# Wider source reads for contiguous loads, and V loads of half the size, in a two-attention kernel

## The chip, the cores and the metric

The kernel runs on one core of one Trainium2 chip. The metric is the device time of one execution in microseconds; a version's time is the median of several executions. A profiled execution also leaves a trace: the instructions of each engine (TensorE for matrix products, called PE in the profile; VectorE, DVE; ScalarE, ACT; GpSimd, POOL; SyncE, SP), the DMA packets, and what released each wait. The core has 16 DMA engines. They move data between main memory (HBM) and the on-chip buffer SBUF, which has 128 partitions; here a partition is also called a row of the destination.

## The reference

Two attention blocks over the same batch shape are computed, and their outputs are laid side by side. Block A has 4 heads of K and V that are shared by 8 query heads each; block B has 32 heads of its own.

```python
def _A_ref(x, k_cache, v_cache, wq, wo):          # x (16, 32, 1024), k and v (16, 4, 1024, 128)
    q = (x @ wq).reshape(B, Sq, 32, 128).transpose(0, 2, 1, 3)
    k = jnp.repeat(k_cache, 8, axis=1)
    v = jnp.repeat(v_cache, 8, axis=1)
    scores = jnp.einsum("bhqd,bhkd->bhqk", q, k) * (128 ** -0.5)
    p = _softmax(scores, axis=-1)
    o = jnp.einsum("bhqk,bhkd->bhqd", p, v)
    return o.transpose(0, 2, 1, 3).reshape(B, Sq, 4096) @ wo
...
a = _A_ref(A_x, A_k_cache, A_v_cache, A_wq, A_wo)
b = _B_ref(B_x, B_k_cache, B_v_cache, B_wq, B_wo)  # the same, with k and v (16, 32, 1024, 128), no repeat
return jnp.concatenate([a, b], axis=-1)            # (16, 32, 2048)
```

All of it is in bfloat16. K and V of block B are 134.2 MB each; K and V of block A, and the query weights and the output weights (both blocks together), are 16.8 MB each. Nearly all of the 338 MB that are read is read once.

## The kernel before

Work is cut into 128 steps. A step of block B ("quad B") takes two batches and two heads: 32 queries of each of the four pairs make the 128 rows of one tile of scores, 128 x 1024. A step of block A ("quad A") takes one batch and four query heads that share one head of K and V. A step in `build` does for B, and likewise for A:

- load K (`st_dmaK`) and V (`st_dmaV`) some steps ahead. For B, K is two loads of 512 KB (L748, one per batch, each partition 4096 B) into one of 8 slots of `KB_sb`, and V two loads of 512 KB (L761, one per batch) into one of 3 slots of `VB_sb`. A load of V for B fills, in each partition, two stretches of 2048 B, one for each head. For A, K (L743, `KA_sb`) and V (L755, `VA_sb`) are one load of 256 KB each, 2048 B to a partition, into one of 2 slots.
- K of B is transposed in place by DVE (L782), K of A by PE (L774);
- scores on PE (L823 for B, L803 for A), the row maximum on DVE (L833), the exponential on ACT (L846), the transpose of P on PE (L858) and its eviction to `PT_sb` (L525);
- P times V on PE (L888 for B, named PVB, four pieces of 32 matmuls in a step; L880 for A), the division by the row sum (L904 on ACT or L905 on DVE), and a transpose of the result on PE (L910).

Between these stand the query projections (L597 and L615, with weights `wq_sb` loaded by L578 as 1024 B pieces) and the output projections (L679), whose weights `woA_sb` and `woB_sb` are loaded by `wo_loadA` and `wo_loadB` (L651 and L661), 256 KB a load, 2048 B to a partition. The results are added up in `acc` by DVE (L690) and stored by L696.

All loads and stores are issued by SP, in one order, on one hardware queue. Where a slot has still to be freed, SP stands at a semaphore wait ahead of that load, and everything behind it stands too. A load's completion adds 16 to its semaphore, one for each DMA engine, and each addition is a 4 B packet.

The order of the instructions on each engine is not written out by hand. `Prog.add` records each operation with what it reads and writes; `list_schedule` then plans them. It picks, engine by engine, among the operations that are ready the one with the longest chain behind it, with planned durations from the table `DUR` and, for a load, from `PACKET`: bytes of a packet and microseconds for it on one DMA engine. Loads follow one another in the plan on one DMA resource, and SP runs at most 5 us (`SP_AHEAD`) ahead of it. The plan sets only orders and buffer numbers; at run time semaphores set when a thing happens. A change of a planned price can thus change the order on every engine.

```python
PACKET = {"kb_dma": (4096, 0.159), "wq_dma": (1024, 0.046)}
PACKET_DEFAULT = (2048, 0.084)
```

Of the kernel before, what the change touches and what calls it, by code (L numbers as in the profile page):

```python
# [6 lines left out]

ALU = alu_op_type.AluOpType
ACTF = mybir.ActivationFunctionType
# [5 lines left out]
HOOK = None  # L15
SCHED = True
NVB_SLOTS = 3
NKB_SLOTS = 8
LAZY_PER_STEP = 100
LAZY_DELAY = 4  # L20
# [24 lines left out]
    "c0": (0.2, 0.1), "c1": (0.3, 0.1),  # L45
}

PACKET = {"kb_dma": (4096, 0.159), "wq_dma": (1024, 0.046)}
PACKET_DEFAULT = (2048, 0.084)
DMA_ISSUE = 0.45  # L50
DMA_FIRST = 1.4
# [3 lines left out]
def dma_time(op):  # L55
    size, us = PACKET.get(op.name, PACKET_DEFAULT)
    return op.dur / size * us / 16
# [373 lines left out]
def build(nc, pa, pb, out):  # L431
    P = 128
# [5 lines left out]
    Dh = pa["k"].shape[3]  # L438
    Sk = pa["k"].shape[2]
    assert Dh == P and Sk == 1024  # L440
    NCH = Sk // P
# [4 lines left out]
    MS = 4  # L446
    NVB = NVB_SLOTS
    NKB = NKB_SLOTS
    HqA = pa["wq"].shape[1] // Dh
# [14 lines left out]
    pr = Prog()  # L464
    stack = contextlib.ExitStack()
    with stack:
        def sb(name, shape, dt):
            return stack.enter_context(nc.sbuf_tensor(name, shape, dt))
# [15 lines left out]
        woA_sb = sb("woA_sb", [P, HS, D], BF)  # L484
        woB_sb = sb("woB_sb", [P, MS, D], BF)
# [4 lines left out]
        VB_sb = sb("VB_sb", [P, NVB, 2, 2, NCH, Dh], BF)  # L490
        KA_sb = sb("KA_sb", [P, 2, NCH, Dh], BF)
        VA_sb = sb("VA_sb", [P, 2, NCH, Dh], BF)
# [8 lines left out]
        def bank(v):  # L501
            return ps_g[:, v.idx, :]
# [4 lines left out]
        if HOOK is not None:  # L507
# [4 lines left out]
               reads=["zeros"], writes=["ident"], name="c1")  # L512
        pr.add("pool", lambda g: g.memset(z32[:], 0.0), writes=["z32"], name="c0")
        pr.add("pool", lambda g: g.affine_select(id32[:], z32[:], [[1, P]], ALU.not_equal, 1.0, base=0, channel_multiplier=-1),
               reads=["z32"], writes=["id32"], name="c1")

        def evac(dst_ap, src_ap, reads, writes, name, eng=None, wtag=None, rtag=None, mul=None):
            def emit(e):
                dst = dst_ap() if callable(dst_ap) else dst_ap
                src = src_ap() if callable(src_ap) else src_ap  # L520
                if mul is not None:
                    if hasattr(e, "activation"):
                        return e.activation(dst, src, ACTF.Copy, scale=mul)
                    return e.tensor_scalar(dst, src, mul, None, ALU.mult)
                return e.copy(dst, src) if hasattr(e, "activation") else e.tensor_copy(dst, src)  # L525
            eng = eng or "any"
            pr.add(eng, emit, reads=reads, writes=writes, name=name if eng == "any" else name + "@" + eng, wtag=wtag, rtag=rtag)
# [26 lines left out]
        def lazy_push(key, thunk):  # L554
            lazy.append((key, thunk, cur_step[0] + LAZY_DELAY))
# [50 lines left out]
        def qprojB(m_, G):  # L606
            lazy_flush(("wq", 1, m_))

            JS = 2 if DJ % 2 == 0 else 1
            v = Virt("bank", "pj")  # L610
            for j0 in range(0, DJ, JS):
                def e_qp(e, j0=j0):
                    last = None
                    for j in range(j0, j0 + JS):
                        last = e.matmul(bank(v)[:, 0:CW], xT_sb[:, 1, j, G * P:(G + 1) * P], wq_sb[:, 1, j, :], start=(j == 0), stop=(j == DJ - 1))  # L615
                    return last
                pcs = sorted(set(j * WQP // DJ for j in range(j0, j0 + JS)))
                pr.add("pe", e_qp, reads=[("wq", 1, k_) for k_ in pcs] + [("xT", 1, G)], writes=[v], claims=[("Qtok", m_ % 2, G)], name="qprojB", dur=0.225 * JS,
                       rtag=dict((("wq", 1, k_), m_) for k_ in pcs))
            evac(Qtok[:, m_ % 2, G, :], lambda: bank(v)[:, 0:CW], reads=[], writes=[v, ("Qtok", m_ % 2, G)], name="qB_ev",  # L620
                 wtag={("Qtok", m_ % 2, G): m_}, mul=scale)
# [23 lines left out]
        def wo_loadA(s_):  # L645
            wo = pa["wo"]
            for h_ in range(HS):
                r0 = (s_ * HS + h_) * Dh

                def th(h_=h_, r0=r0):  # L650
                    pr.add("sp", lambda e: e.dma_start(woA_sb[:, h_, :], wo[r0:r0 + Dh, :]),  # L651
                           writes=[("woA", h_)], dma_key=f"woA{h_}", name="woA_dma", dur=Dh * D * 2, wtag={("woA", h_): s_})
                lazy_push(("wo", 0, s_), th)

        def wo_loadB(m_):
            wo = pb["wo"]
            for h_ in range(MS):
                r0 = (m_ * MS + h_) * Dh

                def th(h_=h_, r0=r0):  # L660
                    pr.add("sp", lambda e: e.dma_start(woB_sb[:, h_, :], wo[r0:r0 + Dh, :]),  # L661
                           writes=[("woB", h_)], dma_key=f"woB{h_}", name="woB_dma", dur=Dh * D * 2, wtag={("woB", h_): m_})
                lazy_push(("wo", 1, m_), th)

# [73 lines left out]
        def st_dmaK(q, t_=None):  # L738
            if q.pi == 0:
                if not q.kv_new:  # L740
                    return
                sl = q.kvslot
                pr.add("sp", lambda e: e.dma_start(KA_sb[:, sl, :, :], pa["k"][q.b, q.s].rearrange("(p c) d -> p c d", c=NCH)),  # L743
                       writes=[("KA", sl)], dma_key=f"ka{sl}", name="ka_dma", dur=Sk * Dh * 2, wtag={("KA", sl): q.kid})
            else:
                sl = q.ks[t_]
                ksrc = pb["k"][q.b0 + t_, q.h0:q.h0 + 2].rearrange("hh (p s) d -> (hh p) (s d)", s=16)
                pr.add("sp", lambda e: e.dma_start(KB_sb[:, sl, :], ksrc), writes=[("KB", sl)], dma_key=f"kb{sl}", name="kb_dma", dur=2 * Sk * Dh * 2, wtag={("KB", sl): q.kid})  # L748

        def st_dmaV(q):  # L750
            if q.pi == 0:
                if not q.kv_new:
                    return
                sl = q.kvslot
                pr.add("sp", lambda e: e.dma_start(VA_sb[:, sl, :, :], pa["v"][q.b, q.s].rearrange("(p c) d -> p c d", c=NCH)),  # L755
                       writes=[("VA", sl)], dma_key=f"va{sl}", name="va_dma", dur=Sk * Dh * 2, wtag={("VA", sl): q.kid})
            else:
                sl = q.vslot
                for t_ in range(2):
                    vsrc = pb["v"][q.b0 + t_, q.h0:q.h0 + 2].rearrange("hh (p c) d -> p hh c d", c=NCH)  # L760
                    pr.add("sp", lambda e, t_=t_, vsrc=vsrc: e.dma_start(VB_sb[:, sl, t_, :, :, :], vsrc), writes=[("VB", sl, t_)],  # L761
                           dma_key=f"vb{sl}_{t_}", name="vb_dma", dur=2 * Sk * Dh * 2, wtag={("VB", sl, t_): q.kid})

        def st_ktrA(q):
            if not q.kv_new:
# [101 lines left out]
        def ptc_of(vPT, c, lo, hi):  # L867
            return PT_sb[:, vPT.idx, :, :].rearrange("p c q -> p (c q)").rearrange("p (m r two) -> p m r two", m=NPK, two=2)[:, c // 2, lo:hi, c % 2]

        def st_pv(q):  # L870
            vPT, vb = q.vPT, q.vbo
            gp = ((q.s if q.pi == 0 else q.m) * NG + q.G) % 2
            heads = [q.hh0 + a_ for a_ in range(4)] if q.pi == 0 else [2 * q.hp, 2 * q.hp + 1]
            ot = [("OT", q.pi, gp, h_) for h_ in heads]
            kvs = q.kvslot if q.pi == 0 else q.vslot
            if q.pi == 0:
                def e_pv(e):
                    last = None
                    for c in range(NCH):
                        last = e.matmul(bank(vb)[:, 0:Dh], ptc_of(vPT, c, 0, P), VA_sb[:, kvs, c, :], start=(c == 0), stop=(c == NCH - 1))  # L880
                    return last
                pr.add("pe", e_pv, reads=[vPT, ("VA", kvs)], writes=[vb], claims=ot, name="PVA", rtag={("VA", kvs): q.kid})
            else:
                def e_pv(e, c0):
                    last = None
                    for c in range(c0, c0 + 2):
                        for a in range(4):
                            last = e.matmul(bank(vb)[32 * a:32 * a + 32, 0:Dh], ptc_of(vPT, c, 32 * a, 32 * a + 32), VB_sb[:, kvs, a // 2, a % 2, c, :],  # L888
                                            start=(c == 0), stop=(c == NCH - 1), tile_position=(0, 32 * a))
                    return last  # L890
                for c0 in range(0, NCH, 2):
                    pr.add("pe", lambda e, c0=c0: e_pv(e, c0), reads=[vPT, ("VB", kvs, 0), ("VB", kvs, 1)], writes=[vb], claims=ot, name="PVB",
                           dur=0.2, tag="B%d" % q.t, rtag={("VB", kvs, 0): q.kid, ("VB", kvs, 1): q.kid})

        def st_recip(q):
            vst = q.vst
# [182 lines left out]
        if SCHED:  # L1079
            pr = pr.list_schedule()  # L1080
# [41 lines left out]
```

## Time and profile before

| what | value |
|---|---|
| median of 3 executions | 897.84 us (897.69 to 898.4) |
| the profiled execution's own time | 897.88 us |
| its span, first to last instruction | 896.0 us |
| HBM read / written | 337.64 MB / 2.10 MB, 379 GB/s over the span |
| mean granted clock of TensorE | 0.992 |
| DVE, K transposes of B, L782 | 256 x 1228 ns = 309.8 us busy; idle before them 30.3 us, 28.6 of it for the load of K |
| DVE, row maximum, L833 | 256 x 1206 ns = 304.4 us busy |
| ACT, exponential, L846 | 256 x 1121 ns = 286.4 us busy |
| PE, transposes of P, L858 | 1024, 174.0 us busy |
| PE, P times V of B, L888 | 4096, 93.1 us busy |
| SP, issues of V of B, L761 | 256, shortest 367 ns, median 474, longest 4105 |
| SP, issues of K of B, L748 | 256, shortest 328 ns, median 615, longest 3368 |

The trace holds one record for each DMA packet. By size, over the whole execution:

| bytes | records | mean ns | median ns | what they are |
|---|---|---|---|---|
| 4 | 12,545 | 9.2 | 9 | semaphore additions |
| 1024 | 16,384 | 49.7 | 47 | query weights |
| 2048 | 92,160 | 88.5 | 86 | V of B (65,536), K of A, V of A and output weights (8,192 each), inputs and outputs (2,048) |
| 4096 | 32,768 | 164.7 | 164 | K of B |
| 8192 | 32 | 379.4 | 345 | instruction fetches, on another queue |
| 16384 | 102 | 1085.7 | 1094 | instruction fetches, on another queue |

How to read the rest: times of engines are busy times. PE's matmuls are pipelined and their ends are modelled, so a share near 100% is not PE at its peak. The DMA share is the packets' time over 16 engines' time; it can pass 100% because the records of neighbouring packets overlap a little. "us to landing" is from the start of the issue on SP to the last semaphore addition.

### The profile page before, as it was taken

To read this page: it belongs to the slowest core of one execution; us is meant where nothing else is said; L and a number is where in the kernel's file an instruction comes from. 1 tells how busy PE (TensorE), PEld (TensorE's weight loads), DVE (VectorE), ACT (ScalarE), POOL (GpSimd) and SP (SyncE) were. 2 spreads that over 40 slices of the span, in tenths; PEclk is the share of its full clock that TensorE was granted. 3 is DMA by queue.
4 is the path that set the end of the run, shared out by engine and by line. 5 is a ranking of instruction groups with operands and counts; after the bars stand their busy time and mean duration, and the time that the engine had idled before them with its cause. 6 is when DMAs were issued, how large, how long until landed. Compare 5 with 4: busy or idle time off the path is not lost.

```text
span 896.0 us, 29282 instructions
## 1 busy us (share of the span) xinstructions
PE 813.8 (91%) x12693; PEld 476.3 (53%) x12864; DVE 740.8 (83%) x1047; ACT 611.8 (68%) x1394; POOL 1.1 (0%) x8
## 2 busy tenths in 40 slices
PE   7999999999999999999889999999989988988876
PEld 4355555555555555555545555555546555555543
DVE  0679888879988898878998788888889789898975
ACT  3468877768777576776767576775768767676752
POOL 0000000000000000000000000000000000000000
PEclk9999999999999999999999999999999999999989
DMA  9999999999999999999999999999999999999994
GB/s 324 386 387 394 395 391 385 382 396 389 388 387 390 395 395 378 385 394 395 394 365 388 392 395 396 379 386 394 393 387 372 392 395 394 396 394 395 397 368 145
DMA packets 153983, 341.66 MB, mean 381 GB/s; under 512 B 12544, under 2 KB 28928, under 8 KB 153856
## 3 DMA queue, kind: packets, MB, share of 16 engines
q1 hardware_dynamic: 153856, 339.79, 101.1%
q8 instruction: 101, 1.65, 0.8%
q14 instruction: 26, 0.21, 0.1%
HBM read 337.64 MB, written 2.10 MB: 379 GB/s over the span
## 4 chain that ended last, share of the span: by engine, by line
PE 51%; DMA 18%; DVE 16%; ACT 9%; SPq 3%; issue 3%; DVEq 0%; ACTq 0%
PE ps_s L823 11%; PE ps_g L858 9%; DMA KB_sb<-in_B_k_cache_dram 8%; PE ps_g L679 8%; DVE stat L833 7%; DVE KB_sb L782 5%; ACT P_sb L846 5%; PE ps_g L888 5%; DMA wq_sb<-in_A_wq_dram 4%; PE ps_g L880 4%; PE ps_g L597 4%; PE ps_g L615 3%; DMA VA_sb<-in_A_v_cache_dram 3%; PE ps_s L803 2%; PE ps_g L774 2%
## 5 line engine op out<-in xcount | busy, mean ns | idle before, releaser
L833 DVE TENSOR_REDUCE stat<-ps_s 128x1 f32<-128x1024 f32 x256 | 304.4, 1206 | 48.0 <-PE ps_s L823 33.8
L782 DVE STREAM_TRANSPOSE KB_sb<-KB_sb 128x1024 f32<-128x1024 f32 x256 | 309.8, 1228 | 30.3 <-DMA KB_sb<-in_B_k_cache_dram 28.6
L846 ACT ACTIVATE P_sb<-ps_s,stat 128x1024 bf16<-128x1024 f32 x256 | 286.4, 1121 | 66.8 <-DVE stat L833 63.7
L858 PE MATMUL ps_g<-id,P_sb 128*128 128x128 f32 x1024 | 174.0, 296 | 14.0 <-ACT QR L525 4.5
L858 PEld LDWEIGHTS ps_g<-id,P_sb 128*128 128x128 f32 x1024 | 151.0, 207 | 53.5 <-ACT QR L525 7.4
L823 PE MATMUL ps_s<-KB_sb,QR 32*32 32x512 bf16 x4096 | 161.9, 400 | 15.7 <-ACT P_sb L846 10.7
L525 ACT COPY PT_sb<-ps_g 128x512 f32<-128x512 f32 x232 | 133.6, 594 | 43.8 <-PE ps_g L858 43.0
L904 ACT ACTIVATE O_sb<-ps_g,stat 128x128 bf16<-128x128 f32 x173 | 63.0, 372 | 58.9 <-PE ps_g L888 35.3
L888 PE MATMUL ps_g<-VB_sb,PT_sb 128*32 128x128 bf16 x4096 | 93.1, 221 | 4.6 <-ACT PT_sb L525 1.5
L888 PEld LDWEIGHTS ps_g<-VB_sb,PT_sb 128*32 128x32 bf16 x4096 | 59.3, 96 | 53.4 <-issue 37.9
L823 PEld LDWEIGHTS ps_s<-KB_sb,QR 32*32 32x32 bf16 x4096 | 46.6, 89 | 74.6 <-ACT P_sb L846 17.5
L880 PE MATMUL ps_g<-VA_sb,PT_sb 128*128 128x128 bf16 x1024 | 78.9, 220 | 2.8 <-DMA VA_sb<-in_A_v_cache_dram 1.7
L880 PEld LDWEIGHTS ps_g<-VA_sb,PT_sb 128*128 128x128 bf16 x1024 | 60.6, 98 | 30.3 <-issue 10.3
L615 PE MATMUL ps_g<-wq_sb,xT_sb 128*128 128x512 bf16 x223 | 67.2, 389 | 5.5 <-issue 2.5
L803 PE MATMUL ps_s<-KTA_sb,QT_sb 128*128 128x512 bf16 x182 | 66.5, 384 | 5.5 <-ACT P_sb L846 1.5
L597 PE MATMUL ps_g<-xT_sb,wq_sb 128*128 128x512 bf16 x232 | 65.8, 380 | 5.4 <-issue 1.9
L679 PE MATMUL ps_g<-woB_sb,OTB_sb 128*128 128x512 bf16 x229 | 62.0, 380 | 4.9 <-issue 2.3
L679 PE MATMUL ps_g<-woA_sb,OTA_sb 128*128 128x512 bf16 x243 | 61.0, 380 | 2.7 <-issue 1.3
L910 PE MATMUL ps_g<-ident,O_sb 128*128 128x128 bf16 x256 | 49.9, 222 | 7.6 <-ACT O_sb L904 2.6
L525 ACT CAST QR<-ps_g 128x256 bf16<-128x256 f32 x117 | 43.7, 382 | 18.4 <-PE ps_g L637 14.3
L690 DVE TENSOR_TENSOR acc<-acc,ps_g 128x512 f32<-128x512 f32 x64 | 41.5, 678 | 13.1 <-PE ps_g L679 12.8
L846 ACT ACTIVATION_READ_ACCUMULATOR P_sb<-ps_s,stat 128x1 f32 x256 | 52.1, 204 | 0.0
(40 smaller groups left out, 528.2 us busy)
## 6 DMA issues: line engine op xcount, KB each, us to landing
VB_sb<-in_B_v_cache_dram SPq DMA_DIRECT2D x256, 512.0 KB, 10.9
KB_sb<-in_B_k_cache_dram SPq DMA_DIRECT2D x256, 512.0 KB, 12.1
KA_sb<-in_A_k_cache_dram SPq DMA_DIRECT2D x64, 256.0 KB, 11.1
VA_sb<-in_A_v_cache_dram SPq DMA_DIRECT2D x64, 256.0 KB, 11.4
wq_sb<-in_B_wq_dram SPq DMA_DIRECT2D x32, 256.0 KB, 10.1
wq_sb<-in_A_wq_dram SPq DMA_DIRECT2D x32, 256.0 KB, 9.7
woB_sb<-in_B_wo_dram SPq DMA_DIRECT2D x32, 256.0 KB, 11.1
woA_sb<-in_A_wo_dram SPq DMA_DIRECT2D x32, 256.0 KB, 9.8
```

Source lines behind the costliest of these rows:

```text
L525: return e.copy(dst, src) if hasattr(e, "activation") else e.tensor_copy(dst, src)
L597: last = e.matmul(bank(v)[:, 0:tn], wq_sb[:, 0, j, hc * Dh:(hc + 1) * Dh], xT_sb[:, 0, j, t0:t0 + tn], start=(j == 0), stop=(j == DJ - 1))
L615: last = e.matmul(bank(v)[:, 0:CW], xT_sb[:, 1, j, G * P:(G + 1) * P], wq_sb[:, 1, j, :], start=(j == 0), stop=(j == DJ - 1))
L679: last = e.matmul(bank(v)[:, 0:OUTW], OT[:, gp, hh, :], wo_[:, hh, oh * OUTW:(oh + 1) * OUTW], start=(hh == 0), stop=(hh == nh - 1))
L782: pr.add("dve", lambda e: e.transpose(KB_sb[:, sl, :].bitcast(F32), KB_sb[:, sl, :].bitcast(F32)), writes=[("KB", sl)], name="KBt_tr", rta ...
L803: pr.add("pe", lambda e, u=u: e.matmul(ps_s[:, vS.idx, u, :], qt[:, q.b, q.hh0:q.hh0 + 4, :].rearrange("p a q -> p (a q)"), KTA_sb[:, sl, ...
L823: last = e.matmul(ps_s[32 * cg:32 * cg + 32, vS.idx, g2, :].rearrange("p (s j) -> p s j", s=16), lhsT, rhs, start=(fp == 0), stop=(fp == 3 ...
L833: pr.add("dve", lambda e: e.tensor_reduce(stat[:, vst.idx, 0:1], ps_s[:, vS.idx, :, :], AXIS.XY, ALU.max, negate=True), writes=vS.res + [v ...
L846: return e.activation(dst, src, ACTF.Exp, bias=stat[:, vst.idx, 0:1], scale=1.0, accum_out=stat[:, vst.idx, 1:2])
L858: last = e.transpose(bank(vb)[:, m * P:(m + 1) * P], p32[:, m:Sk // 2:NPK], id32[:])
L880: last = e.matmul(bank(vb)[:, 0:Dh], ptc_of(vPT, c, 0, P), VA_sb[:, kvs, c, :], start=(c == 0), stop=(c == NCH - 1))
L888: last = e.matmul(bank(vb)[32 * a:32 * a + 32, 0:Dh], ptc_of(vPT, c, 32 * a, 32 * a + 32), VB_sb[:, kvs, a // 2, a % 2, c, :], start=(c == ...
```

## The change

A new function `load` builds the DMA instruction itself. Its destination is as before, 128 partitions with 2048 B in each; its source is given as 32 stretches of 8192 B (`ROWS = 4`), which in memory lie one behind the other. So 16 DMA engines have two source stretches and eight destination rows each, for every 256 KB. K and V of A and the output weights of both blocks go through it, with the same 256 KB to a load as before. V of B goes through it one head at a time: four loads of 256 KB in a step where there were two of 512 KB, two of them on one semaphore; a PVB matmul group waits for all four. K of B, the query weights, the inputs and the stores stay as they were.

The planner's prices for the loads that use it are changed too, from the default (2048 B in 0.084 us) to those of K of B (4096 B in 0.159 us), 0.0410 to 0.0388 ns per byte on one DMA engine.

```diff
+ROWS = 4
...
-PACKET = {"kb_dma": (4096, 0.159), "wq_dma": (1024, 0.046)}
+PACKET = {"kb_dma": (4096, 0.159), "vb_dma": (4096, 0.159), "ka_dma": (4096, 0.159), "va_dma": (4096, 0.159), "woA_dma": (4096, 0.159), "woB_dma": (4096, 0.159), "wq_dma": (1024, 0.046)}
...
+        def load(e, dst, src, rows):
+
+            n = dst.shape[1]
+            d_ = AP(dst.tensor, dst.offset, [list(dst.ap[0]), [1, n]])
+            s_ = AP(src.tensor, src.offset, [[rows * n, P // rows], [1, rows * n]])
+            return e.add_instruction(mybir.InstDMACopy(name=nc.get_next_instruction_name(), mode="Copy", engine=mybir.EngineType.SP,
+                                                       ins=e.lower_ap_dma(s_), outs=e.lower_ap_dma(d_), queue="qSPDynamicHW"))
...
-                    pr.add("sp", lambda e: e.dma_start(woA_sb[:, h_, :], wo[r0:r0 + Dh, :]),
+                    pr.add("sp", lambda e: load(e, woA_sb[:, h_, :], wo[r0:r0 + Dh, :], ROWS),
...
-                pr.add("sp", lambda e: e.dma_start(KA_sb[:, sl, :, :], pa["k"][q.b, q.s].rearrange("(p c) d -> p c d", c=NCH)),
+                pr.add("sp", lambda e: load(e, KA_sb[:, sl, :, :].rearrange("p c d -> p (c d)"), pa["k"][q.b, q.s], ROWS),
...
                 for t_ in range(2):
-                    vsrc = pb["v"][q.b0 + t_, q.h0:q.h0 + 2].rearrange("hh (p c) d -> p hh c d", c=NCH)
-                    pr.add("sp", lambda e, t_=t_, vsrc=vsrc: e.dma_start(VB_sb[:, sl, t_, :, :, :], vsrc), writes=[("VB", sl, t_)],
-                           dma_key=f"vb{sl}_{t_}", name="vb_dma", dur=2 * Sk * Dh * 2, wtag={("VB", sl, t_): q.kid})
+                    for hh in range(2):
+                        pr.add("sp", lambda e, t_=t_, hh=hh: load(e, VB_sb[:, sl, t_, hh, :, :].rearrange("p c d -> p (c d)"), pb["v"][q.b0 + t_, q.h0 + hh], ROWS),
+                               writes=[("VB", sl, t_, hh)], dma_key=f"vb{sl}_{t_}", name="vb_dma", dur=Sk * Dh * 2, wtag={("VB", sl, t_, hh): q.kid})
...
-                    pr.add("pe", lambda e, c0=c0: e_pv(e, c0), reads=[vPT, ("VB", kvs, 0), ("VB", kvs, 1)], writes=[vb], claims=ot, name="PVB",
-                           dur=0.2, tag="B%d" % q.t, rtag={("VB", kvs, 0): q.kid, ("VB", kvs, 1): q.kid})
+                    pr.add("pe", lambda e, c0=c0: e_pv(e, c0), reads=[vPT] + [("VB", kvs, x // 2, x % 2) for x in range(4)], writes=[vb], claims=ot, name="PVB",
+                           dur=0.2, tag="B%d" % q.t, rtag=dict((("VB", kvs, x // 2, x % 2), q.kid) for x in range(4)))
```

The same replacement is made for `woB_sb` and `VA_sb`.

## The prediction

> **What bounds the kernel now.** I read the page's slices of the span first, then its DMA queues, then the stretches of the trace, the waits, the DMA issues and the chain.
>
> ```profile
> span 896.0 us, 29282 instructions
> PE 813.8 (91%) x12693; PEld 476.3 (53%) x12864; DVE 740.8 (83%) x1047; ACT 611.8 (68%) x1394; POOL 1.1 (0%) x8
> ...
> DMA  9999999999999999999999999999999999999994
> ...
> q1 hardware_dynamic: 153856, 339.79, 101.1%
> ...
> PE 51%; DMA 18%; DVE 16%; ACT 9%; SPq 3%; issue 3%; DVEq 0%; ACTq 0%
> ```
>
> The DMA engines are full from the first slice to the last but one; the queue's packets alone take 101.1% of sixteen engines' span (neighbours overlap a little). PE is busy too, 813.8 us. The chain of waits names PE oftener than DMA, but it steps through whoever released last; it does not say whose work could not have been done sooner. So I cut the steady part into stretches of 50 us (columns: length, busy us of PE, PEld, DVE, ACT, POOL, then clock, DMA share, GB/s):
>
> ```profile
> 150.00:200.00 50.00, 47.69 (x747) 27.70 (x756) 39.94 (x57) 36.97 (x86) 0.00 (x0) 1.00 1.03 388
> ...
> 650.00:700.00 50.00, 44.30 (x716) 27.33 (x726) 45.54 (x66) 35.64 (x85) 0.00 (x0) 1.00 1.03 381
> 700.00:750.00 50.00, 45.15 (x767) 27.20 (x774) 42.70 (x63) 35.45 (x81) 0.00 (x0) 1.00 1.04 394
> ...
> sum 800.00, PE 740.67 PEld 437.53 DVE 692.49 ACT 570.89 POOL 0.00; mean PE 46.29 PEld 27.35 DVE 43.28 ACT 35.68 POOL 0.00
> ```
>
> From 50 to 850 us the DMA share is 1.03 or 1.04 in every stretch, while PE goes from 95.4% (47.69 of 50) down to 86.8%. DMA is the one resource that never has room, and PE stands close behind: 740.67 of 800 us, 92.6%. Last, who holds SP up (us in total, times, longest), and how long a load takes:
>
> ```profile
> SPq L761 <- PE ps_g L888: 88.0, 36, 5.4
> SPq L761 <- PE ps_s L823: 84.9, 34, 7.1
> ...
> SPq L748 <- PE ps_g L679: 1.9, 3, 1.4
> ```
> ```profile
> VB_sb<-in_B_v_cache_dram SPq DMA_DIRECT2D x256, 512.0 KB, 10.9
> KB_sb<-in_B_k_cache_dram SPq DMA_DIRECT2D x256, 512.0 KB, 12.1
> KA_sb<-in_A_k_cache_dram SPq DMA_DIRECT2D x64, 256.0 KB, 11.1
> ```
>
> A 512 KB load is 1.35 us of traffic at 389 GB/s, and 10.9 us pass from issue to landing; a load of half the size takes no less. Some 9 to 10 us of work stand in the queue, so SP's waits for free V slots, at most 7.1 us, leave no hole in the DMA.
>
> **The change, part by part.** *Wider reads.* 65,536 rows of VB (134.2 MB), 8,192 each of KA, VA and the output weights (16.8 MB each) are 90,112 packets of 2048 B now; they become 22,528 reads of 8192 B over the same addresses, each with four destination rows. The trace's packet records give means of 49.7 ns at 1024 B, 88.5 at 2048 and 164.7 at 4096 (shortest common values 46, 84, 159): some 9 to 12 ns per packet besides the bytes. No packet of before reads 8192 B for four rows, so I bound it. Best case, the straight line through 2048 and 4096: 164.7 + 2 x 76.2 = 317.1 ns against 4 x 88.5 = 354, so 22,528 x 36.9 / 16 = 52.0 us saved. Worst case, the 32 packets of 8192 B on another queue (instruction fetches), 379.4 ns: 25.4 ns dearer, 35.8 us lost. Between them lies no saving, if each 2048 B write keeps the fixed time. I take the pace of the K loads of B, 164.7 per 4096 B or 329.4 per 8192 B, because these packets are nearest in bulk and destination, and the four writes may keep part of the fixed time: 22,528 x 24.6 / 16 = 34.6 us saved.
>
> The Trainium skill ("DMA: Bandwidth & Descriptors", Why small descriptors are slow) puts the overhead at about three cycles per packet and finds joining worth it only at 256 B and below, which speaks against the change. With the 850 MHz of its section Where 436 GB/s comes from, three packets saved are an estimated 10.6 ns per wide read, 14.9 us in all, instead of 34.6. The trace disagrees on the size: 2 x 84 - 159 = 9 ns per packet, not 3.5.
>
> *V of B in 256 KB loads.* 256 loads more, each with 16 semaphore packets of 4 B (9.2 ns; 12,545 such records now): 256 x 16 x 9.2 / 16 = 2.4 us of DMA. On SP the 784 issues take 636 us in sum, 0.33 to 0.47 us each where nothing holds them back; 256 more at 0.43 are 110 us. They hide in the 294 us by which today's issues exceed 0.45 us because the queue is full, and in SP's waits. With that cover gone they would cost up to 110 us. Every V wait is on the first of the four loads, so none is added there.
>
> The same page (Rules for kernel authors) asks for 1 MiB or more per load. By its fit of 2.0 us plus bytes over 436 GB/s, halving 256 loads adds an estimated 512 us if they ran one by one; the trace disagrees, since loads overlap and the DMA share does not fall below 1.03 in these stretches.
>
> *A new order.* The planner's prices for these loads fall by 5%, so every engine's order is new. On SP the built order has K loads of B waiting for PE at 83 places, 13 before: loads now stand earlier relative to the scores that free their slot. Behind such a wait stand the next V loads, and for those the PVB matmuls. Three such waits now take 1.9 us; 70 more at 0.6 are 42 us of SP time, covered by the 9 us backlog. At the start the four first K loads move ahead of six V loads (4.92 us of issue); DVE waits 7.64 us for K at 26.8 us, but the scores at 32.0 also wait for the projection on PE, so I take nothing. Bounds: one wait of the longest kind each way, 7.1 us.
>
> *The sum.* DMA alone: 896.0 - 34.6 + 2.4 = 863.8 us. That asks PE to do its 740.67 us in 800 - 32.2 x 800/870 = 770 us, 96.1%; no 50 us stretch has passed 95.4%, though the best 20 us reach 97.5% (19.49 of 20, at 360). I hold PE to 95.4%: 740.67 / 0.954 = 776.4 us, 23.6 less than now. So 8.6 us of the DMA's gain are lost to PE, and the span is 872.4. This execution took 897.88 us, 1.9 over its span and 0.04 over the median: **874 us**. Its own range: from 858 (the straight line for the reads, with PE at 97.5%: 740.67 / 0.975 = 760, so 856 + 1.9) to 881 (the order's 7.1 us against it).
>
> **The rivals.**
> 1. *The wide read is dearer.* One read feeding four writes may stall the engine; it decides from 352 ns per read on (354 less 1.7 for the semaphores). At 379.4 ns: 897.8 + 35.8 + 2.4 = 936 us. For: the only 8192 B records are slow (median 345, some 568). Against: their shortest is 307, on the straight line, and they run beside the full queue.
> 2. *Nothing is saved*, because the hardware cuts the reads at the 2048 B rows anyway, or because the writes hold all the fixed time: the change then doesn't do what it says. 897.8 + 2.4 = 900 us, give or take the order. For: no record separates read from write.
> 3. *Half is saved*, 12.3 ns per wide read: 17.3 - 2.4 = 14.9, so 883 us. Both sides of a copy may have their own fixed time.
> 4. *DMA gains all of it and PE follows.* Straight line: 52.0 - 2.4 = 49.6, so 848 us. Against: PE at 98%, above any 20 us seen. For: matmul ends are modelled, so 95% is no hard wall.
> 5. *SP's queue becomes the bound.* If the 42 us of new K waits come through as empty DMA: 863.8 + 42 + 1.9 = 908 us. It decides when SP stands for longer than the backlog, some 9 us. Against: the longest wait now is 7.1 us. For: a faster DMA drains that backlog.
>
> **How the numbers follow.** Forecast 0.50, dearer read 0.17, nothing 0.10, half 0.10, all of it 0.06, SP 0.07. What a measurement of this kernel tells from no change is 0.2%, 1.8 us. Faster: 0.50 + 0.10 + 0.06 = 0.66. The "nothing" case lies at the edge, half of it same: 0.05. Slower: 0.17 + 0.07 + 0.05 = 0.29. The range from 848 to 908 us leaves out the dearer read and a little at the ends, 0.2.
>
> **What would show it.** The packet count falls from 153,856 to about 90,400 (67,584 fewer reads, 4,096 semaphore packets more), if a packet is recorded by its read, and a record of 8192 B near 329 ns stands where 2048 was. GB/s in the steady slices rises from 389 to about 400. The DMA share falls below 1.03 in some stretches and PE's rises towards 95%; DVE's 28.6 us of waits for K of B shrink. Loads land sooner than 10.9 us. If packets stay at 2048 B, rival 2 holds; if the 8192 B records pass 352 ns, rival 1. If DMA has holes while SP waits on PE with PE below 93%, it is rival 5. The forecast is wrong if PE stays at 92.6% and DMA at 1.04.

## The result, and the profile after

The changed kernel takes 902.1 us (median of 4, 901.5 to 903.1) against 897.9 for the kernel before in the same runs: a ratio of 1.0053, interval 1.004 to 1.0065. It is slower by 4 to 6 us where 874 was forecast. Lines of code stand ten lines lower in the changed kernel (scores of B L833, P times V of B L898, output projections L689, K loads of B L758, stores L706); every load that goes through `load` shows as L524.

From its page, the slices, the DMA queue and the chain:

```profile
span 899.3 us, 29687 instructions
...
PE 836.4 (93%) x12864; PEld 478.0 (53%) x12864; DVE 747.7 (83%) x1069; ACT 607.3 (68%) x1372; POOL 1.1 (0%) x8
...
DMA  9999999999999999999999999999999999999993
...
q1 hardware_dynamic: 90368, 339.81, 99.1%
...
PE 54%; DMA 23%; DVE 11%; ACT 7%; SPq 3%; issue 1%; DVEq 0%
```

Packets fell from 153,856 to 90,368, so the hardware does read 8192 B at a time. Their time fell by 2% of the engines' span, and yet the execution is longer. The stretch from 50 to 800 us, first of the kernel before, then of the changed one (columns: length, busy us of PE, PEld, DVE, ACT, POOL, clock, DMA share, GB/s), says why that is no contradiction:

```profile
50.00:800.00 750.00, 697.27 (x11074) 410.77 (x11225) 646.42 (x913) 535.85 (x1234) 0.00 (x0) 1.00 1.04 389
```
```profile
50.00:800.00 750.00, 713.31 (x11188) 409.48 (x11189) 651.29 (x932) 529.06 (x1203) 0.00 (x0) 1.00 1.02 389
```

The same 389 GB/s, with a DMA share of 1.02 instead of 1.04. The records became shorter and overlap less; no more bytes pass. By the packet records the two kernels have moved 269.0 and 269.1 MB at 700 us, and 308.2 MB each at 800. All of the loss comes after that. The next 50 us, before and changed:

```profile
800.00:850.00 50.00, 43.40 (x762) 26.76 (x768) 46.06 (x69) 35.04 (x82) 0.00 (x0) 0.97 1.04 395
```
```profile
800.00:850.00 50.00, 44.48 (x742) 26.77 (x731) 44.84 (x68) 33.20 (x77) 0.00 (x0) 0.93 1.00 382
```

At 850 us the changed kernel is 0.7 MB behind, an estimated 1.8 us at 389 GB/s; the rest is lost later. (PE's 697.27 counts 11,074 matmuls for 11,225 weight loads: the trace before lacks some 150 matmul records in this stretch, 171 in all, and PE was busier than it showed.)

The packet records of 8192 B have a mean of 341.5 ns and a median of 336 (22,562 of them, 34 of these instruction fetches), those of 4096 B 165.5. Loads land sooner, and K loads wait for PE as the order said:

```profile
KB_sb<-in_B_k_cache_dram SPq DMA_DIRECT2D x256, 512.0 KB, 9.8
VB_sb<-in_B_v_cache_dram SPq DMA_DIRECT2D x512, 256.0 KB, 8.0
```
```profile
SPq L524 <- PE ps_s L833: 91.9, 48, 5.4
SPq L524 <- PE ps_g L898: 66.1, 46, 5.7
...
SPq L758 <- PE ps_g L898: 9.6, 12, 2.8
```

All waits of L758 for PE come to 46 us now, at 70 places (7 us at 10 places before), and the DMA share stays at 1.00 or above in every 50 us stretch to 850 us.

### The profile page after: what moved, and what is told of

Read it like the earlier page. It is cut to its first block, busy times and chain, and to the rows that moved or that the text cites. A ratio compares the mean times of both kernels' runs of the same rounds, so it can differ in the third digit from the quotient of the medians.

```text
span 899.3 us, 29687 instructions
## 1 busy us (share of the span) xinstructions
PE 836.4 (93%) x12864; PEld 478.0 (53%) x12864; DVE 747.7 (83%) x1069; ACT 607.3 (68%) x1372; POOL 1.1 (0%) x8
## 3 DMA queue, kind: packets, MB, share of 16 engines
q1 hardware_dynamic: 90368, 339.81, 99.1%
## 4 chain that ended last, share of the span: by engine, by line
PE 54%; DMA 23%; DVE 11%; ACT 7%; SPq 3%; issue 1%; DVEq 0%
DMA KB_sb<-in_B_k_cache_dram 15%; PE ps_s L833 10%; PE ps_g L868 9%; PE ps_g L689 9%; PE ps_g L898 5%; DVE KB_sb L792 5%; ACT P_sb L856 4%; DVE stat L843 4%; PE ps_g L607 4%; PE ps_s L813 4%; PE ps_g L890 4%; PE ps_g L625 3%; DMA woB_sb<-in_B_wo_dram 3%; DMA wq_sb<-in_A_wq_dram 3%; SPq L524 2%; PE ps_g L784 2%
## 5 line engine op out<-in xcount | busy, mean ns | idle before, releaser
L833 PE MATMUL ps_s<-KB_sb,QR 32*32 32x512 bf16 x4096 | 163.7, 395 | 16.1 <-ACT P_sb L856 9.9
L535 ACT COPY PT_sb<-ps_g 128x512 f32<-128x512 f32 x224 | 130.3, 591 | 42.0 <-PE ps_g L868 40.7
L914 ACT ACTIVATE O_sb<-ps_g,stat 128x128 bf16<-128x128 f32 x187 | 67.2, 369 | 70.6 <-PE ps_g L898 47.5
L898 PE MATMUL ps_g<-VB_sb,PT_sb 128*32 128x128 bf16 x4096 | 95.8, 223 | 5.8 <-issue 1.7
L813 PE MATMUL ps_s<-KTA_sb,QT_sb 128*128 128x512 bf16 x256 | 92.2, 387 | 0.9 <-ACT P_sb L856 0.4
L898 PEld LDWEIGHTS ps_g<-VB_sb,PT_sb 128*32 128x32 bf16 x4096 | 60.5, 97 | 59.7 <-issue 43.5
L833 PEld LDWEIGHTS ps_s<-KB_sb,QR 32*32 32x32 bf16 x4096 | 46.5, 89 | 73.8 <-ACT P_sb L856 25.4
L625 PE MATMUL ps_g<-wq_sb,xT_sb 128*128 128x512 bf16 x256 | 76.2, 389 | 2.7 <-DMA wq_sb<-in_B_wq_dram 1.8
L607 PE MATMUL ps_g<-xT_sb,wq_sb 128*128 128x512 bf16 x256 | 71.6, 381 | 3.9 <-ACT QR L535 0.9
L689 PE MATMUL ps_g<-woB_sb,OTB_sb 128*128 128x512 bf16 x256 | 70.2, 387 | 4.8 <-DMA woB_sb<-in_B_wo_dram 3.4
L689 PE MATMUL ps_g<-woA_sb,OTA_sb 128*128 128x512 bf16 x256 | 63.0, 380 | 2.4 <-ACT OTA_sb L535 2.3
```

Source lines behind the costliest of these rows:

```text
L607: last = e.matmul(bank(v)[:, 0:tn], wq_sb[:, 0, j, hc * Dh:(hc + 1) * Dh], xT_sb[:, 0, j, t0:t0 + tn], start=(j == 0), stop=(j == DJ - 1))
L689: last = e.matmul(bank(v)[:, 0:OUTW], OT[:, gp, hh, :], wo_[:, hh, oh * OUTW:(oh + 1) * OUTW], start=(hh == 0), stop=(hh == nh - 1))
L813: pr.add("pe", lambda e, u=u: e.matmul(ps_s[:, vS.idx, u, :], qt[:, q.b, q.hh0:q.hh0 + 4, :].rearrange("p a q -> p (a q)"), KTA_sb[:, sl, ...
L833: last = e.matmul(ps_s[32 * cg:32 * cg + 32, vS.idx, g2, :].rearrange("p (s j) -> p s j", s=16), lhsT, rhs, start=(fp == 0), stop=(fp == 3 ...
```

## The experiments

Ratios are to the kernel before, run on the same chip beside each. A is the theory that the wide read moves nothing faster; B that it does, and the order hides it; C that it costs; D that the order costs all along the run.

| run | what it is | time, us | ratio, 95% interval |
|---|---|---|---|
| changed | wide reads, split V, new prices | 902.1 | 1.0053 (1.004 to 1.0065) |
| e1_narrow | changed, reads of 2048 B | 902.1 | 1.0047 (1.0031 to 1.0062) |
| e2_oldprice | changed, old planner prices | 893.3 | 0.9956 (0.994 to 0.9972) |
| e3_priceonly | before, new planner prices | 898.1 | 1.0007 (0.9998 to 1.0016) |
| e10_inorder_wide | order of before, wide reads, split V | 897.9 | 0.9998 (0.9989 to 1.0007) |
| e11_inorder_narrow | order of before, split V | 897.6 | 0.9995 (0.9984 to 1.0007) |
| e12_after_stores | changed, stores last | 898.7 | 1.0012 (1.0 to 1.0023) |
| e14_before_stores | before, stores last | 895.6 | 0.9974 (0.9963 to 0.9985) |
| e15_after_tail | changed, late projections put off | 892.5 | 0.993 (0.9916 to 0.9943) |
| e16_tail_narrow | the same, reads of 2048 B | 892.7 | 0.9944 (0.9932 to 0.9957) |
| e17_before_tail | before, late projections put off | 897.8 | 1.0002 (0.9993 to 1.001) |
| e13_oldprice_stores | wide, split, old prices, stores last | 891.3 | 0.9915 (0.9901 to 0.993) |
| e18_old_stores_tail | the same, late projections put off | 891.5 | 0.9938 (0.9924 to 0.9952) |

**Is the wide read worth anything?** First, in the changed kernel's own order:

```diff
-ROWS = 4
+ROWS = 1
```

> The changed kernel with ROWS = 1: same loads of 256 KB, same planner prices, same order on every engine, but each load reads 2048 B for each destination row as before. Theory A (the full queue moves the same bytes per second whatever the size of the read; the loss is from the order and from the 256 loads more): within 3 us of the changed kernel, 899 to 905, and GB/s in the steady stretches the same 386. Theory B (the wide read saves what its records show, 341.5 against 4 x 88.5 ns, 17.6 us of DMA time, and the order or SP takes it back): about 12 to 18 us slower than the changed kernel, 914 to 920. Theory C (the wide read is itself what costs): faster than the changed kernel, 896 to 899.

902.1 us, as the changed kernel. That speaks for A and against C. B predicted 914 or more. The cost was then measured by itself, with streams of loads and nothing else:

```diff
+def narrow(dst, i):
+    return raw(e, dst, 0, [[1, 1024]], head(v, i), 0, [[1024, 128], [1, 1024]])
+def wide(dst, i):
+    return raw(e, dst, 0, [[1, 1024]], head(v, i), 0, [[4096, 32], [1, 4096]])
...
+def k_wide(dst, i):
+    return raw(e, dst, 0, [[1, 2048]], pair(k, i), 0, [[4096, 64], [1, 4096]])
```

> No attention at all: SP alone streams V and K of B through 16 slots, in eight stages of 41.9 MB each: 2048 B reads, 8192 B reads over four rows, 4096 B over two rows, 512 KB loads of two heads, K rows of 4096 B, 8192 B over two rows of 4096 B, and the first two again. The output holds some K and V, not the attention. Theory A: stages of 2048 B, 4096 B and 8192 B reads into 2048 B rows run within 1.5% of one another, near 390 GB/s, about 107 us each; K rows at most 1% better. Theory B: the 8192 B stage is faster by 3 to 7%, 405 to 418 GB/s, about 101 to 104 us. Theory C: it is slower than the 2048 B stage by over 2%.

The middles of its eight stages, in the order of the expectation (columns: length, POOL, clock, DMA share, GB/s):

```profile
10.00:105.00 95.00, 0.00 (x0) 1.00 1.05 387
125.00:215.00 90.00, 0.00 (x0) 1.00 1.02 387
240.00:330.00 90.00, 0.00 (x0) 1.00 1.03 387
350.00:440.00 90.00, 0.00 (x0) 1.00 1.05 387
465.00:545.00 80.00, 0.00 (x0) 1.00 1.03 410
570.00:655.00 85.00, 0.00 (x0) 1.00 1.02 410
675.00:765.00 90.00, 0.00 (x0) 1.00 1.05 388
790.00:880.00 90.00, 0.00 (x0) 1.00 1.02 387
```

Reads of 2048, 8192, 4096 and again 2048 B (two heads to a load) into rows of 2048 B: 387 GB/s each. Rows of 4096 B: 410, whether read by 4096 or by 8192 B. So with rows of 2048 B the size of the read does nothing. A missed one thing: K rows are 6% better, not 1%. That the destination row sets the pace is the nearest reading, but the streams alone do not show it: every stage with rows of 4096 B also loads K, every other one V, and V was not loaded into rows of 4096 B. The kernel before speaks for the row: the median records of 1024, 2048 and 4096 B there (47, 86 and 164 ns), from different tensors, leave the same 8 ns beside the bytes at each doubling. The DMA share tells reads apart (1.05 against 1.02) where the bytes do not.

Then the same question with the kernel's order held still. Here V of B goes out as two loads under one operation of the planner, so that every engine's order is that of before:

```diff
+                for x in (last if isinstance(last, list) else [last]):
+                    x.then_inc(sems[op.dma_key], 16)
...
-lambda e, t_=t_, vsrc=vsrc: e.dma_start(VB_sb[:, sl, t_, :, :, :], vsrc)
+lambda e, t_=t_: [load(e, VB_sb[:, sl, t_, hh, :, :].rearrange("p c d -> p (c d)"), pb["v"][q.b0 + t_, q.h0 + hh], ROWS) for hh in range(2)]
```

> The kernel of before with its own order on every engine kept exactly: planner prices and operations as before, but each V load of B is issued as two loads of 256 KB one behind the other, and these, K and V of A and the output weights read 8192 B over four rows. Theory A (the destination row of 2048 B sets the pace, so the wide read is worth nothing; what the changed kernel loses lies in its order near the end): 897.7 to 900.1, the 2.4 us of semaphore packets at most. Theory B (the wide read saves DMA time, hidden in the changed kernel by its order): 880 to 890.

> As the run with the order of before kept, but reads of 2048 B: V of B in two loads of 256 KB, nothing wide. Theory A: within 1.5 us of the wide one, 897.7 to 900.1. Theory B: 8 to 18 us slower than the wide one.

897.9 and 897.6, neither told apart from before, and outside B's 880 to 890. Wide reads and 256 loads more are each worth nothing in this order; of the 2.4 us for semaphore packets nothing shows (by e11's interval 0.6 us at most).

**Does the order cost, and where?** The planner's prices alone, and the change without them:

```diff
-PACKET = {"kb_dma": (4096, 0.159), "wq_dma": (1024, 0.046)}
+PACKET = {"kb_dma": (4096, 0.159), "vb_dma": (4096, 0.159), "ka_dma": (4096, 0.159), "va_dma": (4096, 0.159), "woA_dma": (4096, 0.159), "woB_dma": (4096, 0.159), "wq_dma": (1024, 0.046)}
```

> The kernel of before with the changed planner prices alone; reads of 2048 B and V in 512 KB loads. Theory A: DMA unchanged, so only the order shows: 898 to 903, with the loss of the changed kernel if the order makes it (about 900), 897.9 if it does not. Theory B: the order costs what the wide reads gain, so about 12 to 18 us slower than before, 910 to 916.

> The changed kernel with the planner's prices of before; wide reads and the split V loads stay. Theory A, if the new order is what costs: back to 897.9 + 2.4 (4 B packets) = about 900 or less. If the order costs nothing, 902 as changed. Theory B: the order of before with the wide reads' gain, below 890.

The prices alone change nothing (898.1); without them the change makes the kernel faster (893.3); with both it is slower. No single part carries a loss: each gives the planner another order. Between e2 and before the operations differ in the two V loads, and e10 shows that the loads themselves are worth nothing, so its 4.4 us are an order's too.

Where an order matters shows in the chain of the changed kernel, near its end (start us, us, what):

```profile
875.46 5.23 PE ps_g L689 x24
880.69 0.83 PE ps_s L833 x20
...
882.98 0.60 PE ps_g L898 x32
...
886.26 3.85 DMA VB_sb<-in_B_v_cache_dram
890.11 0.14 issue
890.25 0.66 PE ps_g L898 x32
```

and in SP's issues there:

```profile
870.91 5.85 SPq L524 DMA_DIRECT2D VB_sb<-in_B_v_cache_dram  x8
881.01 0.94 SPq L706 DMA_DIRECT2D out_dram<-acc  x2
883.61 3.26 SPq L524 DMA_DIRECT2D VB_sb<-in_B_v_cache_dram  x4
```

PE does 24 output projections in one piece before it turns to the last scores and to the P times V that frees the slot for the last four V loads. SP stands at two stores meanwhile, ahead of those loads. They are issued at 883.6 (the last loads of before: 878.5), and PE waits for them at the end. First the stores, moved behind the last load on SP and nowhere else:

```diff
-        seq = sorted(range(n), key=lambda k: (ops[order[k]].t0, k))
+        seq = sorted(range(n), key=lambda k: (self.specs[order[k]][5] == "out_dma", ops[order[k]].t0, k))
```

> The changed kernel with the eight output stores moved behind the last load in SP's order; the orders of PE, DVE and ACT are the changed kernel's. Theory A, with the place named: SP stands at two stores of A from 876.8 to 881.0 us, ahead of the last four V loads, which are issued at 883.6; without that 4 to 9 us faster than the changed kernel, 893 to 898. Theory D (the order costs in the steady part, by 70 new waits of K loads): unchanged, 900 to 903.

> The kernel of before with its eight output stores moved behind the last load in SP's order, nothing else. Theory A: SP stands some 5 us at a store ahead of the last V loads here too (873.6 to 878.5), so 2 to 8 us faster, 890 to 896. Theory D: unchanged, 897 to 899.

Both gain: the ratio falls by 0.0041 (3.7 us) in the changed kernel, just short of the 4 us that were expected at the least, and by 0.0026 (2.3 us) in the kernel before. So the order of the stores is a loss that both share, and only a small part of the difference. But the place that was named is not where the gain comes from. In the changed kernel the last V loads leave as P times V ends (882.98 + 0.60), after the stores are out, so it is PE that holds them; with the stores behind them they still wait for PE:

```profile
867.82 15.79 SPq L524 DMA_DIRECT2D VB_sb<-in_B_v_cache_dram  x12
883.66 9.67 SPq L706 DMA_DIRECT2D out_dram<-acc  x8
```

Compared weight load by weight load, PE in e12 is 0.1 us ahead of the changed kernel at 800 us, 1.9 at 826 and 3.1 at 871, before SP comes to the two stores, and gains nothing after that. Two things differ up to there. Five stores of 262 KB, issued from 721 to 849 us in the changed kernel, no longer stand ahead of loads, an estimated 3.4 us of traffic at 389 GB/s; and from 800 to 870 us the mean granted clock is 0.95 in e12 and 0.91 in the changed kernel. No run separates the two.

Then the projections, with a lower priority in the plan:

```diff
                            name="oprojA" if pi == 0 else "oprojB",
-                           dur=0.45 * OUTW / 512, rtag=...
+                           prio=-8.0 if blk == nblk - 1 and G >= NG - 2 else 0, dur=0.45 * OUTW / 512, rtag=...
```

> The changed kernel with one priority of the planner lowered: the output projections of the last two groups of each block. Up to row 1,604 of PE's 1,736 (and 433 of SP's 461) the orders are the changed kernel's; after that the 24 projections that stand in one piece of 5.2 us on PE (875.5 to 880.7) ahead of the scores and the P times V of the last steps lie between them, and the last V loads stand ahead of the stores. Theory A (the loss sits in this end): 3 to 7 us faster than the changed kernel, 895 to 899. Theory D (the loss is spread over the steady part): 901 to 903.

892.5 us, 0.993: more than was expected. Its orders are the changed kernel's for the first 92% of PE's rows, up to 810 us, where PE in the two traces is still within 0.8 us, so D falls, and about 10 us (1.0053 less 0.993, and 0.9944 in the narrow version) hang on the last 8%. In the trace the projections now stand in pieces of 2 to 8 between the last steps, and the last four V loads are issued from 872.6 us on, 11 us sooner than in the changed kernel and ahead of the last three stores:

```profile
872.51 0.61 PE L689 MATMUL ps_g<-woA_sb,OTA_sb 128*128 128x512 bf16 x2
872.96 0.63 PE L868 MATMUL ps_g<-id,P_sb 128*128 128x128 f32 x4
...
873.48 1.03 PE L689 MATMUL ps_g<-woA_sb,OTA_sb 128*128 128x512 bf16 x4
```
```profile
867.34 7.67 SPq L524 DMA_DIRECT2D VB_sb<-in_B_v_cache_dram  x8
876.73 10.45 SPq L706 DMA_DIRECT2D out_dram<-acc  x3
```

Two questions were left: whether the wide read shows once the end is free, and whether the kernel before has the same loss there.

> The changed kernel with the lowered priority at its end (892.5 in an earlier run), but reads of 2048 B. Theory A (the wide read is worth nothing in any order): within 1.5 us of that run, 0.991 to 0.995 of the kernel before. Theory B' (a late PE in the changed order and a DMA-bound end hid the wide read's gain, and it shows once the end is free): 3 to 10 us slower, 0.997 or more of the kernel before.

> The kernel of before with the same lowered priority for the last output projections; its orders are those of before up to row 1,563 of PE's 1,682. Theory A: its end is not as bad as the changed kernel's (16 projections in one piece, and the last V loads not waited for), so it gains less than the changed kernel's 1.05%: 892 to 897, 0.993 to 0.999 of before. If the end of the changed kernel is nothing special: the same 0.99.

The narrow reads take 892.7 us with the mended end, the wide ones 892.5: the third pair of equal orders, and the third time no difference. The kernel before gains nothing from the same mending (897.8 where 892 to 897 was expected), which fits its chain: its last V loads are not waited for. What exactly of the end's new order brings the 10 us is not separated further. The 3.7 us of e12 are no part that could be taken off, since five stores stand ahead of the last loads in e15 too. The clock may be a part: from 800 to 870 us it is 0.91 in the changed kernel, 0.93 in the kernel before and 1.00 in e15. Whether it costs there, or only follows from PE's waits, stays open.

**What are the bounds?** Two kernels, each with the orders of before, leave work out:

```diff
-e.dma_start(VB_sb[:, sl, t_, :, :, :], vsrc)
+e.dma_start(VB_sb[:, sl, t_, :, :, :], vsrc) if q.t < NVB else e.dma_start(VB_sb[:, sl, t_, 0:1, 0, :], vsrc[:, 0:1, 0, :])
```

> The kernel of before with its orders, where the V loads of B from the fourth step on fetch 256 B a partition instead of 4096 B, so that P times V of B uses old V data in seven eighths of its input and the output is not the attention. It shows what the other engines need when DMA has room. If DMA alone holds the kernel back: below 870. If PE is the second bound close behind, as its 95.4% in the best stretch said: 860 to 880. If the kernel is bound by its compute order: 890 to 898.

```diff
-                    for j in range(j0, j0 + JS):
+                    for j in range(j0, j0 + 1):
...
-                    for c in range(c0, c0 + 2):
+                    for c in range(c0, c0 + 1):
```

> The kernel of before with its orders and all its loads, where half of the matmuls of both query projections, both output projections and both P times V are left out (every other chunk of the contraction), so the output is not the attention; some 200 us of PE work less. If the DMA rate sets the steady part: within 3 us of 387 GB/s to 850 us, the end a few us earlier, 885 to 895. If PE sets it: below 880 and more GB/s than 397.

From the pages of the first and then the second:

```profile
span 884.9 us, 29453 instructions
...
PE 830.2 (94%) x12864; PEld 476.8 (54%) x12864; DVE 736.4 (83%) x1047; ACT 611.4 (69%) x1394; POOL 1.1 (0%) x8
...
q1 hardware_dynamic: 121856, 216.91, 70.9%
```
```profile
span 892.0 us, 23309 instructions
...
PE 713.1 (80%) x9792; PEld 384.3 (43%) x9792; DVE 740.5 (83%) x1047; ACT 608.3 (68%) x1394; POOL 1.1 (0%) x8
...
q1 hardware_dynamic: 153856, 339.79, 101.2%
```

With 123 MB less to load the kernel of before still needs 885 us of span (886.9 as timed), only 11 us less: its compute, in this order, stands close behind the traffic. The time falls between the second expectation (up to 880) and the third (from 890). With 3,072 matmuls less it needs 892 (894.0): the traffic sets the steady part, 391 GB/s to 800 us. Each is one run.

**The fastest versions.** Both ways of mending, without the planner's new prices:

> Wide reads, split V loads, planner prices of before (893.3 in an earlier run), and the eight stores behind the last load in SP's order. Theory A: another 1 to 4 us, 889 to 892; it would be the fastest so far. Otherwise 892 to 895.

> Wide reads and split V loads, planner prices of before, stores last, and the lowered priority for the last output projections. Theory A: the end is already nearly as short as the traffic lets it be (888.5 us of span with stores last, where the loads end at 874), so 0 to 3 us more, 0.988 to 0.992 of before; the DMA's 870 us of traffic are the floor.

891.3 and 891.5 us, and e15's 892.5 beside them: below both kernels, and close to what the light kernel needed with all its loads. What is left is mostly traffic, by an estimate: 339.8 MB at 389 GB/s are 874 us. e18 missed its bounds (0.9938 where 0.988 to 0.992 was expected): its extra mending gave nothing, and by their ratios it is not better than e13.

## Why the prediction was wrong

- **What bounds the kernel:** right for DMA. From 50 to 800 us the rate was 389 GB/s before, changed, in e1_narrow and in e15 alike, and with PE lightened the span fell by only 4 us.
- **The wide read, -34.6 us:** the step that failed. Its size was the pace of the K loads, "because these packets are nearest in bulk and destination". Their destination row is 4096 B, and loads of K into such rows run at 410 GB/s, whatever the read. With rows of 2048 B the pace stays at 387, and the term of 34.6 us measured 0 (387 and 387 in the streams; 902.1 and 902.1, 897.9 and 897.6, 892.5 and 892.7 in three orders). Beneath it lies a wrong reading: the length of a packet's record was taken for the time that it costs an engine. At 387 GB/s on 16 engines 8192 B take 338.7 ns; four records of 88.5 ns, 354 together, overstate that by 15 ns, the one of 341.5 by 3. So the record of 8192 B did shrink, close to the "half is saved" of rival 3, and it bought no bytes. The DMA share of 1.04 with one queue was the hint: records overlap, so they are no prices.
- **Rival 2, nothing saved:** its second mechanism, that the writes hold all the fixed time, fits the streams; that the wide read saves nothing is shown, why is not. It got 0.10 and the time 900; its 2.4 us for the semaphore packets are not there.
- **The Trainium skill's rule of three cycles a packet** ("DMA: Bandwidth & Descriptors", Why small descriptors are slow): the estimate of 14.9 us that was worked out from it failed as the 34.6 did. The advice of the same section, that joining is worth it only at 256 B and below, agrees with the runs: 902.1 us with wide reads and 902.1 with narrow ones. The same page's wish for loads of 1 MiB (Rules for kernel authors) had no force here: halves of 512 KB loads cost nothing (0.9995).
- **The fit of 2.0 us a load:** the same page of the Trainium skill states it for loads that GpSimd issues (Anatomy of one DMA — SWDGE (gpsimd) path), so it did not bear on these loads, which SP issues.
- **256 loads more on SP:** the cover held. All issues sum to 636 us, as before.
- **The order, "bounds: one wait of the longest kind each way":** wrong in place and cause. The K waits came, 39 us more of them than before where 42 were said, and the backlog hid them, so rival 5 did not happen. The start, taken at nothing, was nothing: at 100 us both kernels have moved 37 MB. But an order's worth was 4.3 us against and 4.4 us for in two versions, and about 10 us hung on the last 8% of the changed kernel's. The prediction looked at SP's waits in the steady part, which has a backlog to hide them, and not at the end, where nothing does.
- **PE held to 95.4%:** the bound was near, but its price was too kind. With the loads out of the way this order needs 885 us of span, not 872, so the forecast could not have been met in that order even with the gain on the reads. PE's share before, 740.67 of 800, was read from a trace that lacked matmul records; the counts, 12,693 for 12,864 weight loads, told of it.
- **The packet count:** 90,368 where about 90,400 was said.
- **The range, 848 to 908 us:** that 902.1 lies in it is luck. Its upper end is rival 5's 908, whose empty DMA did not occur, and no rival had an order that costs at the end.

## What to carry to other kernels

Price a transfer by the bytes that a full queue moves in a stretch of one kind of load, not by the length of its packet records: shorter records can mean less overlap and the same GB/s. On a full queue do not expect a gain from a longer source row alone: here it moved nothing, and the only faster loads had a longer destination row. Where a planner writes the order, every edit of an operation or a price is also a new order: compare in the same order (here two loads under one operation of the planner did it), and read the end of the chain on its own, since the end has no backlog to hide a load that comes late.

## What the hardware showed that was not expected

- One read of 8192 B may feed four rows of 2048 B at no loss and no gain: 387 GB/s. Rows of 4096 B, all of them loads of K, get 410 GB/s from reads of 4096 B and of 8192 B alike.
- An engine's packet records overlap with those of its neighbours, and by how much depends on the form: a DMA share of 1.05 and one of 1.02 both stand for 387 GB/s.
- SP's shortest issue for a load of 256 KB is 0.47 us through `load`, whether it reads 2048 B or 8192 B (e1_narrow and the changed kernel), and was 0.34 for V of A before. No run shows that it changed the time.
